# Turning the first DFT step by DMA transposes inside SBUF in a fused FFT-filter and feed-forward kernel

## The chip, the cores and the metric

The kernel runs on one NeuronCore of one Trainium2 chip. The metric is the device time of one execution in microseconds (us), as the median of several runs. The engines are named as in the profile: PE (TensorE, matrix products), PEld (its weight loads), DVE (VectorE), ACT (ScalarE), POOL (GpSimd) and SP (SyncE, which here only issues DMAs). PE writes to PSUM, from where ACT or DVE must copy the result to SBUF; this copy is called an evacuation below. Sixteen DMA engines move data between DRAM and SBUF and inside SBUF.

## The reference

Two layers, one after the other. The first is a filter in the frequency domain, the second a feed-forward layer with a squared ReLU:

```python
# x: (8, 3008, 256); w_r, w_i: (256, 256); b_r, b_i: (256,)
X = np.fft.rfft(x, axis=1)
Xr, Xi = X.real, X.imag
Yr = Xr @ w_r - Xi @ w_i + b_r
Yi = Xr @ w_i + Xi @ w_r + b_i
Yr = sign(Yr) * max(abs(Yr) - 0.01, 0)      # and Yi likewise
y = np.fft.irfft(Yr + 1j * Yi, n=3008, axis=1)

# y as 24064 tokens of 256; moe_w_in: (256, 2048); moe_w_out: (2048, 256)
h = y @ moe_w_in
g = moe_s * max(h, 0) ** 2 + moe_b
out = g @ moe_w_out
```

## The kernel before

The sequence length is split as 3008 = 94 x 32 (`N1` x `N2`), and the transform is done in two matrix products with constant tables. Per batch there are four steps, all in float16 with float32 accumulation:

- **Step 1** transforms over the 94 values of n1 to 96 rows, which the code counts by kappa (real and imaginary parts of 48 frequencies), for each of the 32 values of n2.
- **Steps 2 and 3** transform over n2 (`F_t`), multiply with the weights (`W_g`, `W_t`), shrink towards zero, and transform back over n2 (`T_t`). They need kappa and n2 together on the partitions: 24 tiles (`NPAIR`) of 128 rows (4 kappa x 32 n2) by 256 columns, held in `us`.
- **Step 4** transforms back over kappa (`C_t`). It needs the 96 kappa rows on the partitions, held in `vs`, and writes `yt`, whose partitions are the model's columns, which is what the feed-forward layer takes as its moving operand.

**Batches 1 to 7.** `s1_units(b)` is a list of 16 units. Before, a unit is one matmul of 94 x 512 with the table `A_t` as the stationary operand (L562), so that kappa comes out on the partitions, and an evacuation of 96 x 512 to `u` (L160 on ACT or L164 on DVE, as `evac` decides by counted loads). After every four units SP writes 384 KB of `u` to a DRAM tensor `ud` (L569); after the sixteenth SP reads it back in four loads with kappa and n2 on the partitions (`us`, L576). So the turn from one layout to the other is made by a trip through DRAM. `s23_units(b)` reads `us` (L598), moves the shrunk values in small copies inside SBUF (`ring`, L647), writes the result `v` to the DRAM tensor `vd` (L666) and reads it back as `vs` in two loads (L673). `s4_units(b)` reads `vs` (L710). x is loaded by POOL in four chunks per batch (`x16`, L189, four buffers), and a chunk's buffer is free again when step 1 of the batch before has read it.

**Batch 0**, in `first_batch`, goes another way, since at the opening there is no other work to lie beside. Step 1 runs with x as the stationary operand (L361), 128 columns at a time, so that the model's columns are on the partitions (`ut`). Then, for each half `ec` of the columns, come six rounds of `mix` (L410), `fwd_dft` (L441) and `inv_dft` (L459), one round behind the other. The result `vt` has the columns on the partitions, and step 4 needs kappa there: `turn` multiplies blocks of `vt` with the identity `eye_t` (L474), eight at a time, and evacuates 96 x 1024 values to `vs`. `last_dft` is step 4 of batch 0 (L491).

**The feed-forward layer** is cut into 48 tiles of tokens, each in 16 slots. A slot has two matmuls of 512 columns with `moe_w_in` (L761), the ReLU on ACT (L768), the square on DVE or ACT (L775, L772), and four matmuls of 256 columns of the tile before with `moe_w_out` (L832). The units of the four steps are put into these slots by `schedule`: step 1 and steps 2 and 3 of a batch lie in the slots of the tiles of earlier batches, about 80 to 96 slots per batch. Each engine runs its instructions in their order in the program; a matmul that waits holds up all matmuls behind it. The order inside the opening is fixed by the loop at the end of `first_batch` and rearranged a little when the program is built.

The pools set how many buffers a name has: `up` 3, `usp` 5 (each a quarter of `us`) and `vsp` 2 (each a half of `vs`) before.

Of the kernel before, what the change touches and what calls it, by code (L numbers as in the profile page):

```python
# [96 lines left out]
def kernel(  # L97
# [29 lines left out]
    sel = np.zeros((P, P))  # L127
    sel[0, :64] = 1.0
    sel[64, 64:] = 1.0
    E_d = nc.inline_tensor(np.eye(P).astype(np.float16), name="identity").ap()  # L130
    S_d = nc.inline_tensor(sel.astype(np.float16), name="bias_sel").ap()

    cpool = ctx.enter_context(tc.tile_pool(name="consts", bufs=1))
# [3 lines left out]
    fpool = ctx.enter_context(tc.tile_pool(name="psf", bufs=2, space=bass.MemoryType.PSUM))  # L137
    dpool = ctx.enter_context(tc.tile_pool(name="dram", bufs=2, space=bass.MemoryType.DRAM))
    xpool = ctx.enter_context(tc.tile_pool(name="xp", bufs=4))
    upool = ctx.enter_context(tc.tile_pool(name="up", bufs=3))  # L140
    uspool = ctx.enter_context(tc.tile_pool(name="usp", bufs=5))
    xfpool = ctx.enter_context(tc.tile_pool(name="xfp", bufs=4))
    mpool = ctx.enter_context(tc.tile_pool(name="mp", bufs=2))
    vpool = ctx.enter_context(tc.tile_pool(name="vp", bufs=3))
    vspool = ctx.enter_context(tc.tile_pool(name="vsp", bufs=2))
    ypool = ctx.enter_context(tc.tile_pool(name="yp", bufs=2))
    tpool = ctx.enter_context(tc.tile_pool(name="tp", bufs=2))
    rpool = ctx.enter_context(tc.tile_pool(name="rp", bufs=3))
# [64 lines left out]
        nc.sync.dma_start(out=st, in_=w.rearrange("(c p) e -> p c e", p=P))  # L213
        w_st.append(st)

    b_g = cpool.tile([P, 2, D], F32, name="b_g")
    nc.vector.memset(b_g, 0.0)
    for r in (0, 64):
        for i, bv in enumerate((b_r, b_i)):
            nc.sync.dma_start(out=b_g[r : r + 1, i], in_=bv.unsqueeze(0))  # L220
    F_c = uspool.tile([P, NPAIR, 2, N2], F16, name="F_c", tag="us")
    b_h = cpool.tile([P, D], F16, name="b_h")
# [4 lines left out]
    sel_t = cpool.tile([P, P], F16, name="sel_t")  # L227
    T_c = uspool.tile([P, NPAIR, 64], F16, name="T_c", tag="us")
    eye_t = cpool.tile([P, P], F16, name="eye_t")
    C_t = cpool.tile([96, 96], F16, name="C_t")  # L230

    b_st = rpool.tile([P, 2, D], F32, name="b_st", tag="rt")
# [12 lines left out]
    def emit_load_inverse():  # L245
        nc.sync.dma_start(
            out=F_c[:, H:].rearrange("p q r k -> p q (r k)"), in_=F_d[:, H:]
        )
        t_load = nc.sync.dma_start(out=T_c, in_=T_d)
        with tc.issue_after(t_load.ins):  # L250
            nc.sync.dma_start(out=eye_t, in_=E_d)
# [24 lines left out]
    F_2 = [uspool.tile([P, H, P], F16, name="F_2", tag="us") for _ in range(2)]  # L276
    for f in F_2:
        nc.gpsimd.memset(f, 0.0)

# [54 lines left out]
    def make_bias():  # L334
        ps = other_bank()
        nc.tensor.matmul(ps[:, 0:D], ones, w_sum, start=True, stop=True)
        for j in range(2):
            nc.scalar.activation(
                out=bias_bc[:, j], in_=ps[:, 0:D], func=AF.Copy, scale=bb_bc
            )  # L340

    us = {}
    vs = {}
    ring = []
# [5 lines left out]
    def first_batch():  # L350
# [46 lines left out]


        U = NPAIR // 4
        vt = bigpool.tile([P, DC, N2, 96], F16, name="vt", tag="corr")  # L400
        gs = {}
        zt = {}
        g_last = [None]
# [61 lines left out]
                ps.rearrange("p (k n) -> p n k", n=N2), 512,  # L465
            )

        for h in range(2):
            vs[(0, h)] = vspool.tile([96, HW, D], F16, name="vs", tag="vs")

        def turn(ec, k):
            ps = two_banks()
            for j in range(8):
                nc.tensor.matmul(  # L474
                    ps[0:96, j // 4, (j % 4) * P : (j % 4) * P + P],
                    vt[:, ec, 8 * k + j, :], eye_t, start=True, stop=True,
                )
            h, n = divmod(8 * k, HW)
            evac(
                vs[(0, h)][:, n : n + 8, ec * P : (ec + 1) * P],  # L480
                ps[0:96].rearrange("p h (j e) -> p (h j) e", e=P), 1024,
            )

        yt = yts[0] = ypool.tile([P, DC, N2, 96], F16, name="yt", tag="yt")

        def last_dft(ec, n2):

            ps = [one_bank(), other_bank()]
            for j in range(8):
                h, k = divmod(n2 + j, HW)  # L490
                nc.tensor.matmul(  # L491
                    ps[j // 4][:, (j % 4) * 96 : (j % 4) * 96 + 96],
                    vs[(0, h)][:, k, ec * P : (ec + 1) * P], C_t,
                    start=True, stop=True,
                )
# [14 lines left out]
        for i in range(2 * U + 2):  # L510
            if i < 2 * U:
                mix(*steps[i])
            if 0 <= i - 1 < 2 * U:
                fwd_dft(*steps[i - 1])
            if 0 <= i - 2 < 2 * U:
                inv_dft(*steps[i - 2])
            k = i - U - 2
            if 0 <= k < 4:
                turn(0, k)
            if 0 <= k - 1 < 4:  # L520
                last_dft(0, 8 * (k - 1))
            if i >= 2 * U:
                some(3)
            if i == 0:
                with tc.issue_after(g_last[0].ins):
                    place_t(0)
            if i == 1:
                with tc.issue_after(g_last[0].ins):
                    place_f(1)
            if i == 2:  # L530
                with tc.issue_after(g_last[0].ins):
                    place_f_2(1)
            if i == 3:
                with tc.issue_after(g_last[0].ins):
                    place_t(1)
            if i == 9:

                gate = nc.gpsimd.tensor_copy(out=low[0:1, 0, 0:1], in_=vt[0:1, 1, 0, 0:1])
                with tc.issue_after(gate.ins):
                    make_w_g()  # L540
                    make_bounds()
                    sum_w_out()
        for k in range(4):
            turn(1, k)
            some(1)
            if k:
                last_dft(1, 8 * (k - 1))
        last_dft(1, 24)
        return more


    def s1_units(b, more_banks=False):

        ud = dpool.tile([96, N2, D], F16, name="ud", tag="ud")
        hold = {}

        def unit(i):
            c, j = divmod(2 * i, XCH)
            if j == 0:
                hold["u"] = upool.tile([P, XCH, D], F16, name="u", tag="u")  # L560
            ps = other_bank() if more_banks and i % 2 else one_bank()
            nc.tensor.matmul(  # L562
                ps[0:96, :], A_t[0:N1, :], x16[(b, c)][0:N1, j * D : (j + 2) * D],
                start=True, stop=True,
            )
            u = hold["u"]
            evac(u[0:96, j : j + 2, :], ps[0:96, :].rearrange("p (j d) -> p j d", j=2), 512)
            if j == XCH - 2:
                nc.sync.dma_start(  # L569
                    out=ud[:, c * XCH : (c + 1) * XCH, :], in_=u[0:96]  # L570
                )
            if i == N2 // 2 - 1:
                uv = ud.rearrange("k n d -> (k n) d").rearrange("(q p) d -> p q d", p=P)
                for q in range(4):
                    t = uspool.tile([P, 6, D], F16, name="us", tag="us")
                    nc.sync.dma_start(out=t, in_=uv[:, 6 * q : 6 * q + 6, :])  # L576
                    us[(b, q)] = t

        return [lambda i=i: unit(i) for i in range(N2 // 2)]

    def s23_units(b):
# [8 lines left out]
        def fwd_unit(i):  # L590

            bank = one_bank()
            ps = bank.rearrange("p (r c j k) -> p r c j k", r=2, c=DC, j=2)
            t = us[(b, i // 3)]
            for j in range(2):
                q = (2 * i + j) % 6
                for dc in range(DC):
                    nc.tensor.matmul(  # L598
                        ps[:, :, dc, j, :], t[:, q, dc * P : (dc + 1) * P],
                        F_t[:, 2 * i + j, :], start=True, stop=True,  # L600
                    )
            xt = xfpool.tile([P, 3, DC, P], F16, name="xf", tag="xf")
# [50 lines left out]
        def inv_unit(i):  # L653
# [14 lines left out]
                )  # L668
            if i == H - 1:
                vv = vd.rearrange("q (k n) e -> (q k) (n e)", n=N2)  # L670
                for h in range(2):
                    t = vspool.tile([96, HW, D], F16, name="vs", tag="vs")
                    nc.sync.dma_start(  # L673
                        out=t.rearrange("k n e -> k (n e)"),
                        in_=vv[:, h * HW * D : (h + 1) * HW * D],
                    )
                    vs[(b, h)] = t

        units = []

# [14 lines left out]
    def s4_units(b):  # L695
# [6 lines left out]
        def unit(g):  # L702
# [3 lines left out]
            yt = yts[b]  # L706
            ps = one_bank()
            for j in range(w):
                h, k = divmod(n2 + j, HW)
                nc.tensor.matmul(  # L710
                    ps[:, j * 96 : (j + 1) * 96],
                    vs[(b, h)][:, k, ec * P : (ec + 1) * P], C_t,
                    start=True, stop=True,
                )
            evac(
# [143 lines left out]
    more = first_batch()  # L859
    load.update(act=0.0, dve=0.0)  # L860
    def load_x_2():
        emit_load_x(2, us[(1, 3)][0:1, 0, 0:1])

    mark = {}
    for i, tl in enumerate(tiles):
        if tl[0] == "main" and tl[2] == 0 or tl[0] == "wide" and tl[2] == (0, 0):
            mark[tl[1]] = i * MC
    schedule(0, 10, more)
    plan.setdefault(15, []).append(make_bias)
    plan.setdefault(17, []).append(load_x_2)  # L870
    schedule(24, 42, s23_units(1))
# [53 lines left out]
```

## Time and profile before

| | |
|---|---|
| median of 3 runs | 852.34 us (851.17 to 854.75) |
| the profiled execution's own time | 851.2 us |
| its span in the profile | 849.4 us |
| mean granted clock of PE | 0.997 |
| busy: PE, DVE, ACT, POOL | 98%, 82%, 76%, 5% |
| HBM read and written | 52.54 MB, 46.66 MB |
| batch 0's dense part (feed-forward matmuls in a row) begins | about 51.5 us |

The span is counted from the first to the last instruction of the core; the run's time is 1.8 us longer. The profile shows busy time by engine, groups of instructions by line, waits with what ended them, a timeline, the chain of work that ended last (followed back from the last instruction), and a table of stretches of time with each engine's busy time, the granted clock, the busy share of the DMA engines and the GB/s that they moved. The ends of matmuls are modelled, so a row's mean duration (382 ns for L562, 205 ns for L710) holds a latency that neighbours overlap; the pace of a run of matmuls is read from the chain.

### The profile page before, as it was taken

The page shows a single profiled execution, that of the slowest core. Times are in us where ns is not written, and L with a number is a line of the kernel's source. Part 1 is how long each engine was busy: PE and PEld are TensorE (multiplying, and loading weights), DVE is VectorE, ACT ScalarE, POOL GpSimd, SP SyncE. Part 2 cuts the span into 40 slices and gives each one's busy share as a digit, 9 for nine tenths or more (in the row PEclk, how much of TensorE's full clock was granted, in tenths as well). Part 3 has the DMA queues.
Part 4 walks back from the last instruction along what each step waited for, and adds up shares of the span by engine and source line. Part 5 has one row for each costly group of instructions (what it writes and reads, how often), then busy time and mean ns, then how long its engine had stood idle before and what let it go on. Part 6 is the DMA issues. An engine that isn't in the chain of part 4 may idle for free.

```text
span 849.4 us, 17085 instructions
## 1 busy us (share of the span) xinstructions
PE 835.0 (98%) x6645; PEld 600.5 (71%) x6645; DVE 697.0 (82%) x1027; ACT 643.2 (76%) x856; POOL 46.6 (5%) x72
## 2 busy tenths in 40 slices
PE   8899999999999999999999999999999999999997
PEld 7757777777677766777677776777667777766765
DVE  6898987888888987888878888888977888776674
ACT  5898887787778787787777887787877787766673
POOL 5321000000000000000000000000000000000000
PEclk9999999999999999999999999999999999999999
DMA  7937457324761367324662247613354223411111
GB/s 165 161 104 162 108 148 185 101 76 100 177 186 54 92 159 184 109 78 103 171 177 65 74 106 199 172 40 92 100 156 118 62 79 98 112 33 38 38 44 50
DMA packets 105458, 95.07 MB, mean 112 GB/s; under 512 B 9510, under 2 KB 97578, under 8 KB 104034
## 3 DMA queue, kind: packets, MB, share of 16 engines
q1 hardware_dynamic: 98930, 79.57, 32.6%
q0 software_dynamic: 6448, 14.42, 10.7%
q8 instruction: 52, 0.85, 0.4%
q14 instruction: 28, 0.23, 0.1%
HBM read 52.54 MB, written 46.66 MB: 117 GB/s over the span
## 4 chain that ended last, share of the span: by engine, by line
PE 88%; DVE 4%; ACT 3%; DMA 2%; issue 1%; POOL 0%; SPq 0%; DVEq 0%; ACTq 0%; POOLq 0%
PE psa L832 36%; PE psh L761 36%; PE psf L627 4%; PE psf L562 2%; PE psf L613 2%; PE psf L598 2%; PE psf L657 2%; PE psf L710 2%; ACT rt L768 1%; DVE gt L775 1%; DMA x<-in_x_dram 1%; DMA out_dram<-ost 1%; PE psh L410 1%; ACT yt L160 0%; ACT vs L160 0%
## 5 line engine op out<-in xcount | busy, mean ns | idle before, releaser
L768 ACT ACTIVATE rt<-psh 128x1024 f32<-128x1024 f32 (+2 forms) x384 | 387.1, 1009 | 119.1 <-PE psh L761 117.7
L775 DVE TENSOR_TENSOR gt<-rt 128x1024 f16<-128x1024 f32 (+2 forms) x321 | 384.0, 1199 | 98.1 <-ACT rt L768 97.4
L832 PE MATMUL psa<-w_out_t,gt 128*128 128x256 f16 (+1 forms) x3024 | 454.3, 272 | 0.1
L832 PEld LDWEIGHTS <-gt 128*128 128x128 f16 (+1 forms) x3024 | 300.9, 101 | 187.2 <-issue 1.7
L761 PE MATMUL psh<-yt,w_in 128*128 128x512 f16 (+1 forms) x1344 | 396.7, 378 | 0.3 <-ACT rt L768 0.3
L761 PEld LDWEIGHTS <-w_in 128*128 128x128 f16 x1536 | 142.9, 98 | 27.4 <-issue 2.1
L842 DVE SCALAR_TENSOR_TENSOR ost<-psa,s_bc,bias_bc 128x512 f32<-128x512 f32 (+2 forms) x97 | 71.0, 732 | 8.3 <-PE psa L832 7.1
L772 ACT ACTIVATE gt<-rt 128x1024 f16<-128x1024 f32 (+2 forms) x63 | 66.2, 1050 | 1.0
L632 DVE TENSOR_TENSOR ring<-psf,s 128x512 f16<-128x512 f32 x84 | 57.5, 684 | 3.7 <-PE psf L627 2.9
L160 ACT CAST v<-psf 128x512 f16<-128x512 f32 x78 | 45.3, 582 | 18.7 <-PE psf L657 18.7
L160 ACT CAST xf<-psf 128x512 f16<-128x512 f32 x82 | 47.9, 585 | 10.9 <-PE psf L598 10.8
L160 ACT CAST u<-psf 96x512 f16<-96x512 f32 x77 | 44.5, 580 | 11.0 <-PE psf L562 10.7
L761 PE MATMUL psh<-tail,w_in 128*128 128x512 f16 (+1 forms) x192 | 52.1, 353 | 0.0
L627 PE MATMUL psf<-W_g,xf 128*128 128x256 f16 x336 | 50.4, 273 | 0.0
L160 ACT CAST yt<-psf 128x480 f16<-128x480 f32 (+2 forms) x75 | 38.1, 520 | 13.6 <-PE psf L710 13.6
L189 POOL DMA_DIRECT2D x<-in_x_dram x36 | 18.9, 530 | 429.3 <-PE psf L562 428.0
L562 PE MATMUL psf<-x,A_t 94*96 94x512 f16 x104 | 39.7, 381 | 1.7 <-ACT yt L160 0.5
L638 DVE TENSOR_TENSOR ring<-ring,high 128x512 f16<-128x512 f16 x84 | 35.5, 423 | 2.3
L639 DVE TENSOR_TENSOR ring<-ring 128x512 f16<-128x512 f16 x84 | 35.5, 422 | 1.9
L637 DVE TENSOR_TENSOR ring<-ring,low 128x512 f16<-128x512 f16 x84 | 35.4, 421 | 1.6
L627 PEld LDWEIGHTS <-xf 128*128 128x128 f16 x336 | 32.9, 98 | 3.8
L710 PE MATMUL psf<-C_t,vs 96*128 96x96 f16 x448 | 33.0, 205 | 0.1
(89 smaller groups left out, 501.9 us busy)
## 6 DMA issues: line engine op xcount, KB each, us to landing
out_dram<-ost SPq DMA_DIRECT2D x152, 128.0 KB
ud<-u SPq DMA_DIRECT2D x28, 384.0 KB
us<-ud SPq DMA_DIRECT2D x28, 384.0 KB
vd<-v SPq DMA_DIRECT2D x42, 256.0 KB
vs<-vd SPq DMA_DIRECT2D x14, 768.0 KB
x<-in_x_dram POOLq DMA_DIRECT2D x28, 376.0 KB, 5.9
ring<-ring SPq DMA_DIRECT2D x280, 32.0 KB
out_dram<-ost SPq DMA_DIRECT2D x16, 120.0 KB
```

The lines of the kernel that those rows point to most:

```text
L160: return None, nc.scalar.copy(out=dst, in_=src)
L562: nc.tensor.matmul(ps[0:96, :], A_t[0:N1, :], x16[(b, c)][0:N1, j * D : (j + 2) * D], start=True, stop=True,)
L627: nc.tensor.matmul(ps[:, r, :], xt[:, 2 - r, dc], W_g[:, dc, r], start=(dc == 0), stop=(dc == DC - 1),)
L632: nc.vector.tensor_tensor(out=t, in0=ps, in1=hold[i // 2][:, i % 2].unsqueeze(1).to_broadcast([P, 2, D]), op=ALU.add,)
L638: nc.vector.tensor_tensor(out=m, in0=m, in1=high, op=ALU.min)
L710: nc.tensor.matmul(ps[:, j * 96 : (j + 1) * 96], vs[(b, h)][:, k, ec * P : (ec + 1) * P], C_t, start=True, stop=True,)
L761: nc.tensor.matmul(o, w_in_t[dc][:, mc * P : (mc + 1) * P], r, start=(dc == 0), stop=(dc == DC - 1),)
L768: nc.scalar.activation(out=rt[:, :, 0:w], in_=ps[:, :, 0:w], func=AF.Relu)
L772: nc.scalar.activation(out=gt[:, :, 0:w], in_=rt[:, :, 0:w], func=AF.Square)
L775: nc.vector.tensor_tensor(out=gt[:, :, 0:w], in0=rt[:, :, 0:w], in1=rt[:, :, 0:w], op=ALU.mult)
L832: nc.tensor.matmul(ps[0:size, h, :], gts[(ti, mc // 2)][:, mc % 2, sub * size : (sub + 1) * size], w_out_t[:, mc, :], start=(mc == 0), sto ...
L842: nc.vector.scalar_tensor_tensor(out=ost[0:size, 0:k], in0=ps[0:size, 0:k], scalar=s_bc[0:size], in1=bias_bc[0:size, 0:k], op0=ALU.mult, o ...
```

## The change

Two places change, and the pools with them.

First, step 1 of batches 1 to 7 takes the form that batch 0 has: x is the stationary operand, four matmuls of 94 x 96 per unit, so that the columns come out on the partitions. A unit now covers four values of n2 and one half `dc` of the columns; the first eight units do the first half, the last eight the second, and each half reads all four chunks of x. `u` holds for each column all 96 x 32 values with kappa outside and n2 inside. After each half, one DMA transpose inside SBUF turns 128 x 3072 values into the 24 tiles of `us`. The DRAM tensor `ud` is gone.

Second, batch 0's `turn` is two DMA transposes of 128 x 2048 values for each half of the columns instead of identity matmuls and evacuations. `vt` is padded to 128 rows for this, and POOL zeroes the padding once. In the loop, `last_dft` of the first half stands three rounds behind the turn; all twelve units of step 1 of batch 1 stand between the second half's turn and its `last_dft`, and the last four between the calls of `last_dft`, so that no unit is left for the slots of the first tile.

The buffers: `us`, `u` and `vs` have one buffer each, for a whole batch; the constants of the opening share the space of `us`, and the bias tables that of `tails`.

```diff
-    E_d = nc.inline_tensor(np.eye(P).astype(np.float16), name="identity").ap()
...
-    upool = ctx.enter_context(tc.tile_pool(name="up", bufs=3))
-    uspool = ctx.enter_context(tc.tile_pool(name="usp", bufs=5))
+    upool = ctx.enter_context(tc.tile_pool(name="up", bufs=1))
+    uspool = ctx.enter_context(tc.tile_pool(name="usp", bufs=1))
...
-    vspool = ctx.enter_context(tc.tile_pool(name="vsp", bufs=2))
+    vspool = ctx.enter_context(tc.tile_pool(name="vsp", bufs=1))
...
+    first_c = uspool.tile([P, 4, NPAIR * 64], F16, name="first_c", tag="us")
+    F_c = first_c[:, 0].rearrange("p (q r k) -> p q r k", q=NPAIR, r=2)
+    T_c = first_c[:, 1].rearrange("p (q k) -> p q k", q=NPAIR)
+    F_2 = [first_c[:, 2 + i].rearrange("p (q k) -> p q k", q=H) for i in range(2)]
...
+    vt = bigpool.tile([P, DC, N2, P], F16, name="vt", tag="corr")
+    nc.gpsimd.memset(vt[:, :, :, 96:P], 0.0)
...
-        def turn(ec, k):
-            ps = two_banks()
+        vs[0] = vspool.tile([P, N2, D], F16, name="vs", tag="vs")
+
+        def turn(ec):
+
+            for k in range(2):
+                nc.sync.dma_start(
+                    out=vs[0][:, HW * k : HW * k + HW, ec * P : (ec + 1) * P],
+                    in_=vt[:, ec, HW * k : HW * k + HW].rearrange("p n k -> p (n k)"),
+                    transpose=True,
+                )
...
             for j in range(8):
                 nc.tensor.matmul(
-                    ps[0:96, j // 4, (j % 4) * P : (j % 4) * P + P],
-                    vt[:, ec, 8 * k + j, :], eye_t, start=True, stop=True,
-                )
-            h, n = divmod(8 * k, HW)
-            evac(
-                vs[(0, h)][:, n : n + 8, ec * P : (ec + 1) * P],
-                ps[0:96].rearrange("p h (j e) -> p (h j) e", e=P), 1024,
-            )
...
-            k = i - U - 2
-            if 0 <= k < 4:
-                turn(0, k)
-            if 0 <= k - 1 < 4:
-                last_dft(0, 8 * (k - 1))
-            if i >= 2 * U:
-                some(3)
+            if i - 1 in (U, 2 * U):
+                turn((i - 1) // U - 1)
+            if 0 <= i - U - 4 < 4:
+                last_dft(0, 8 * (i - U - 4))
...
+        some(12)
         for k in range(4):
-            turn(1, k)
+            last_dft(1, 8 * k)
             some(1)
-            if k:
-                last_dft(1, 8 * (k - 1))
-        last_dft(1, 24)
...
-            ps = other_bank() if more_banks and i % 2 else one_bank()
-            nc.tensor.matmul(
-                ps[0:96, :], A_t[0:N1, :], x16[(b, c)][0:N1, j * D : (j + 2) * D],
-                start=True, stop=True,
-            )
+            for j in range(4):
+                lo = (4 * h + j) * D + dc * P
+                nc.tensor.matmul(
+                    ps[:, j * 96 : j * 96 + 96], x16[(b, c)][0:N1, lo : lo + P],
+                    A_t[0:N1, :], start=True, stop=True,
+                )
...
-                nc.sync.dma_start(
-                    out=ud[:, c * XCH : (c + 1) * XCH, :], in_=u[0:96]
-                )
-            if i == N2 // 2 - 1:
-                uv = ud.rearrange("k n d -> (k n) d").rearrange("(q p) d -> p q d", p=P)
-                for q in range(4):
-                    t = uspool.tile([P, 6, D], F16, name="us", tag="us")
-                    nc.sync.dma_start(out=t, in_=uv[:, 6 * q : 6 * q + 6, :])
-                    us[(b, q)] = t
+                nc.sync.dma_start(
+                    out=us[b][:, :, dc * P : (dc + 1) * P],
+                    in_=u[:, dc].rearrange("p k n -> p (k n)"),
+                    transpose=True,
+                )
...
-    schedule(0, 10, more)
+    assert not more
```

More of the change, by code (lines that the diff above doesn't have):

```diff
@@ L214 @@
         w_st.append(st)
-    b_g = cpool.tile([P, 2, D], F32, name="b_g")
+    b_g = tpool.tile([P, 2, D], F32, name="b_g", tag="tail")
     nc.vector.memset(b_g, 0.0)
@@ L220 @@
             nc.sync.dma_start(out=b_g[r : r + 1, i], in_=bv.unsqueeze(0))
-    F_c = uspool.tile([P, NPAIR, 2, N2], F16, name="F_c", tag="us")
-    b_h = cpool.tile([P, D], F16, name="b_h")
+    first_c = uspool.tile([P, 4, NPAIR * 64], F16, name="first_c", tag="us")
+    F_c = first_c[:, 0].rearrange("p (q r k) -> p q r k", q=NPAIR, r=2)
+    T_c = first_c[:, 1].rearrange("p (q k) -> p q k", q=NPAIR)
+    F_2 = [first_c[:, 2 + i].rearrange("p (q k) -> p q k", q=H) for i in range(2)]
+    sb_t = tpool.tile([P, P + D], F16, name="sb_t", tag="tail")
+    sel_t, b_h = sb_t[:, 0:P], sb_t[:, P:]
     nc.vector.memset(b_h, 0.0)
@@ L226 @@
         nc.gpsimd.dma_start(out=b_h[64 * i : 64 * i + 1], in_=bv.unsqueeze(0))
-    sel_t = cpool.tile([P, P], F16, name="sel_t")
-    T_c = uspool.tile([P, NPAIR, 64], F16, name="T_c", tag="us")
-    eye_t = cpool.tile([P, P], F16, name="eye_t")
     C_t = cpool.tile([96, 96], F16, name="C_t")
@@ L250, in emit_load_inverse @@
         with tc.issue_after(t_load.ins):
-            nc.sync.dma_start(out=eye_t, in_=E_d)
             nc.sync.dma_start(out=C_t, in_=C_d)
@@ L275 @@
     nc.vector.memset(T_t, 0.0)
-    F_2 = [uspool.tile([P, H, P], F16, name="F_2", tag="us") for _ in range(2)]
     for f in F_2:
@@ L399, in first_batch @@
         U = NPAIR // 4
-        vt = bigpool.tile([P, DC, N2, 96], F16, name="vt", tag="corr")
         gs = {}
@@ L466, in inv_dft @@
             )
-        for h in range(2):
-            vs[(0, h)] = vspool.tile([96, HW, D], F16, name="vs", tag="vs")
-        def turn(ec, k):
-            ps = two_banks()
-            for j in range(8):
-                nc.tensor.matmul(
-                    ps[0:96, j // 4, (j % 4) * P : (j % 4) * P + P],
-                    vt[:, ec, 8 * k + j, :], eye_t, start=True, stop=True,
-                )
-            h, n = divmod(8 * k, HW)
-            evac(
-                vs[(0, h)][:, n : n + 8, ec * P : (ec + 1) * P],
-                ps[0:96].rearrange("p h (j e) -> p (h j) e", e=P), 1024,
-            )
+        vs[0] = vspool.tile([P, N2, D], F16, name="vs", tag="vs")
[5 more added lines that the diff above has]
+                    transpose=True,
+                )
         yt = yts[0] = ypool.tile([P, DC, N2, 96], F16, name="yt", tag="yt")
@@ L489, in last_dft @@
             for j in range(8):
-                h, k = divmod(n2 + j, HW)
                 nc.tensor.matmul(
                     ps[j // 4][:, (j % 4) * 96 : (j % 4) * 96 + 96],
-                    vs[(0, h)][:, k, ec * P : (ec + 1) * P], C_t,
+                    vs[0][0:96, n2 + j, ec * P : (ec + 1) * P], C_t,
                     start=True, stop=True,
@@ L542, in first_batch @@
                     sum_w_out()
+        some(12)
         for k in range(4):
-            turn(1, k)
+            last_dft(1, 8 * k)
             some(1)
-            if k:
-                last_dft(1, 8 * (k - 1))
-        last_dft(1, 24)
         return more
     def s1_units(b, more_banks=False):
-        ud = dpool.tile([96, N2, D], F16, name="ud", tag="ud")
         hold = {}
         def unit(i):
-            c, j = divmod(2 * i, XCH)
-            if j == 0:
-                hold["u"] = upool.tile([P, XCH, D], F16, name="u", tag="u")
-            ps = other_bank() if more_banks and i % 2 else one_bank()
-            nc.tensor.matmul(
-                ps[0:96, :], A_t[0:N1, :], x16[(b, c)][0:N1, j * D : (j + 2) * D],
-                start=True, stop=True,
-            )
-            u = hold["u"]
-            evac(u[0:96, j : j + 2, :], ps[0:96, :].rearrange("p (j d) -> p j d", j=2), 512)
-            if j == XCH - 2:
+            dc, g = divmod(i, N2 // 4)
+            if i == 0:
+                hold["u"] = upool.tile([P, DC, 96, N2], F16, name="u", tag="u")
+                us[b] = uspool.tile([P, NPAIR, D], F16, name="us", tag="us")
+            c, h = divmod(g, 2)
+            ps = other_bank() if more_banks and i % 2 else one_bank()
+            for j in range(4):
[4 more added lines that the diff above has]
+                )
+            u = hold["u"]
+            evac(
+                u[:, dc, :, 4 * g : 4 * g + 4],
+                ps[:, 0:384].rearrange("p (n k) -> p k n", k=96), 384,
+            )
+            if g == N2 // 4 - 1:
@@ L593, in fwd_unit @@
             ps = bank.rearrange("p (r c j k) -> p r c j k", r=2, c=DC, j=2)
-            t = us[(b, i // 3)]
             for j in range(2):
-                q = (2 * i + j) % 6
                 for dc in range(DC):
                     nc.tensor.matmul(
-                        ps[:, :, dc, j, :], t[:, q, dc * P : (dc + 1) * P],
+                        ps[:, :, dc, j, :], us[b][:, 2 * i + j, dc * P : (dc + 1) * P],
                         F_t[:, 2 * i + j, :], start=True, stop=True,
@@ L670, in inv_unit @@
                 vv = vd.rearrange("q (k n) e -> (q k) (n e)", n=N2)
+                t = vs[b] = vspool.tile([P, N2, D], F16, name="vs", tag="vs")
                 for h in range(2):
-                    t = vspool.tile([96, HW, D], F16, name="vs", tag="vs")
                     nc.sync.dma_start(
-                        out=t.rearrange("k n e -> k (n e)"),
+                        out=t[0:96, h * HW : h * HW + HW].rearrange("k n e -> k (n e)"),
                         in_=vv[:, h * HW * D : (h + 1) * HW * D],
                     )
-                    vs[(b, h)] = t
         units = []
@@ L708, in unit @@
             for j in range(w):
-                h, k = divmod(n2 + j, HW)
                 nc.tensor.matmul(
                     ps[:, j * 96 : (j + 1) * 96],
-                    vs[(b, h)][:, k, ec * P : (ec + 1) * P], C_t,
+                    vs[b][0:96, n2 + j, ec * P : (ec + 1) * P], C_t,
                     start=True, stop=True,
@@ L861, in load_x_2 @@
     def load_x_2():
-        emit_load_x(2, us[(1, 3)][0:1, 0, 0:1])
+        emit_load_x(2, us[1][0:1, 0, 0:1])
     mark = {}
```

## The prediction

> **What bounds the kernel now.** I read the chain of work that ended last first. It says which engine a saved instruction must sit on to be worth anything.
>
> ```profile
> PE 88%; DVE 4%; ACT 3%; DMA 2%; issue 1%; POOL 0%; SPq 0%; DVEq 0%; ACTq 0%; POOLq 0%
> ```
>
> PE carries 88% of the end, DMA 2%. So the first step's trip through DRAM (`ud`, `us`), which the change removes, costs nothing today; only PE work counts there. What that work costs is read from the chain in order of time, where neighbours do not overlap:
>
> ```profile
> 51.21 0.22 PE psf L562
> ...
> 243.69 0.43 PE psf L710 x10
> ```
>
> A first-step matmul over 512 columns takes 0.22 us (217 ns over many). The last step's 96-column matmul, with a weight load for each, goes ten in 0.43 us, 43 ns each: the shape that the changed first step will have.
>
> The windows of the opening come next, since batch 0 has nothing beside it to hide in:
>
> ```profile
> 8.00:12.00 4.00, 3.66 (x43) 3.55 (x42) 1.92 (x5) 2.52 (x6) 2.75 (x3) 0.57 1.10 200
> ...
> 28.00:32.00 4.00, 3.86 (x48) 3.22 (x47) 2.73 (x5) 3.59 (x6) 0.00 (x0) 1.00 1.08 216
> 32.00:36.00 4.00, 3.72 (x55) 3.42 (x53) 3.47 (x5) 3.32 (x6) 3.06 (x4) 1.00 1.36 193
> 36.00:40.00 4.00, 3.93 (x60) 3.55 (x58) 3.77 (x6) 3.41 (x7) 2.68 (x4) 1.00 0.71 96
> ```
>
> The last column but one is the DMA share: the 16 DMA engines are full until about 39 us (the weights of the second part and batch 1's x), just when batch 0's first turn will be asked for. The column before it is the granted clock; after the waits on x it fell to 0.57.
>
> Last, the timeline of SP and PE in batch 3's first step, for what a transpose may take before somebody waits:
>
> ```profile
> 241.88 0.31 SPq L569 DMA_DIRECT2D ud<-u  x1
> ...
> 247.67 2.55 SPq L576 DMA_DIRECT2D us<-ud  x4
> ```
> ```profile
> 253.26 0.39 PE L598 MATMUL psf<-F_t,us 128*128 128x128 f16 x4
> ```
> ```profile
> 250.00:255.00 5.00, 5.00 (x41) 3.72 (x39) 3.85 (x4) 3.27 (x5) 0.70 (x1) 1.00 0.95 268
> ```
>
> From the end of the first step to the first reader of `us` are 11.4 us (12.2 in batch 2, 16 to 18 in others). The window is the reload of `us` in 512-byte pieces: 268 GB/s at 95%.
>
> **The first step of batches 2 to 7.** Out: 16 matmuls of 217 ns, 3.47 us. In: 64 of 43 ns, 2.75 us. Gain 0.72 us a batch, 4.3 us for six, all on PE. The evacuations shrink from 582 to 479 ns on ScalarE and from 681 to 558 on VectorE (rows of `u` now and of batch 0's `ut`, which has the new form); neither is the bound. The DRAM copies go, worth nothing.
>
> **The price of a DMA transpose.** No row of before shows one. Below: as fast as the fastest copy, 268 GB/s, so 2.0 us for one of batch 0's four (128 x 2048, 524 KB) and 2.9 us for one of a later batch's two (128 x 3072, 786 KB). Middle: each 128-element row of a block is a piece of its own and costs what a 512-byte piece costs in that window, 16 x 512 B / 268 GB/s = 30.6 ns on one of 16 engines: 128 pieces, 3.9 us, and 192 pieces, 5.9 us. Above: each such row cut in eight, 31 and 47 us. I take the middle, because the pieces of a transpose must be at least as many as those of the plain copy nearest to it, and keep both ends. To each comes some 2 us from issue to landing that bytes don't explain (the `vd` write of 256 KB issued at 222.4 us was waited for until 226.6, of which 1 us is bytes; I take less, as that one had a queue ahead).
>
> The page "DMA: Bandwidth & Descriptors" of the Trainium skill, section "Latency and other measured facts", gives 261 GB/s for a DMA transpose; by it the lower end holds. The page "VectorE: DVE Perf Modes", section "The three transpose paths", speaks against the change: 1309 ns for a 128 x 128 block by DMA against 390 on TensorE, and it prefers TensorE where PSUM will do. Block after block that would be 21 and 31 us, and a total beyond 1000 us as an estimate. Here TensorE turned eight blocks in 0.46 us (`turn` L474 in the chain), 57 ns each, plus an evacuation of 1.0 to 1.2 us for the eight.
>
> **Batch 0, the opening.** The 64 identity matmuls and eight evacuations go (about 8.5 us of ScalarE and VectorE together); an opening step falls from 2.4 to 1.73 us (the inverse matmuls stand at 26.33, 28.06 and 29.79 us before any turn, then 31.75, 34.19, 36.54). By the order of the changed program the first reader of the turned rows stands after three more such steps: 29.79 + 3 x 1.73 + 0.2 = 35.2 us. The transpose is issued when the last `vt` is written, 31.45 us. With the engines full until 39.6 us (when POOL's wait for `w_out_t` at L327 ends) and shared with the weights, 3.9 us become about 7, and with 2 us the first half lands at 40.8: PE, in order, stands 5.6 us with the rest of the opening behind it. The second half: 46.5 us, against 44.8 when PE gets there, 1.7 more. Then the last `vt` at 47.7, the other transposes from there, landing at 53.6 and 57.5. Twelve units of batch 1's first step cover 3.3 us of it (12 evacuations of 0.48 and 0.56 on two engines), so PE waits from 51.0 to 53.6 and, after 1.5 us of work, from 55.1 to 57.5; 1.5 us more and the dense part begins at 59.0. Before, it ran from 51.5. That is +7.5 us. Six first-step units that lay in the first tile move ahead of it; the tile is paced by ScalarE, three of its 0.6 us evacuations go: -1.8. The stalls should cost clock too (the 0.57 window): I take +1.0. Opening: +6.7 us.
>
> **What is newly late in the dense part.** Two things. The old order read a chunk of x once, so the next batch's load could start after four units; the new one reads each chunk again for the second half of the columns, so all four loads (4.1 to 10.4 us each, off the path today: POOL's wait for L562 is 428 us and nobody waits for POOL) crowd into the second half of the step, beside the `vs` reload (issued 226.6, read from 236.2 us) and the second transpose. And the first transpose stands on SP ahead of the last two `vd` writes and the `vs` reload, which wait behind its 5.9 us. The second has 2 + 5.9 = 7.9 us against 11.4: it fits, unless it shares the engines with a load (13.8, 2 us late in batches 2 and 3). I charge 1.0 for that and 1.5 for `vs`. `us`, `u` and `vs` with one buffer cost nothing: their last readers are over 10 us back; if the transposes grew past 9 us, that cover would go first.
>
> The rest is free: the extra memset of `vt` on POOL (some 2 us by the 1.4 us row of 1536 columns) ends before POOL's gate at 16.7 us; the constants in other pools move no copy that is waited for.
>
> **Sum.** -4.3 + 6.7 + 1.0 + 1.5 = +4.9 on the profiled run's own 851.2 us (span 849.4): 856.1. The median of the runs is 1.1 above that run: 857.
>
> **Rivals.** (1) Transposes at copy speed, faster: the lower end. First half at 31.45 + 2 + 4 = 37.5, second at 43.6, the other two at 48.8 and 50.8, dense part from 52.3: +0.8 - 1.8 = -1.0; in the dense part nothing is late but 0.5; total -4.8, so 847.5 by the median. For it: 268 GB/s is reached by 512-byte pieces here. Against: a transpose scatters each piece over partitions. (2) The weights hold the DMA engines and copy speed gives back only PE's gain less the stall: no change, 849 to 855; it decides where one of batch 0's transposes takes about 3 us. (3) The transposes are long and become the bound: at 8 us (12 for a later batch) the opening adds about 25 us and each batch some 2, 885 us; past 11 us for a later one, `vs` and `us` are late in every batch by twice the excess, and at 31 and 47 us the total is some 1300. For it: a 16-bit transpose writes short runs. Against: no row. That the change does not do what it says is out: the changed program has four transposes of 128x16x128 and fourteen of 128x24x128 on SP, no identity matmul and no `ud`.
>
> **How the numbers follow.** About 0.5% is what a measurement here tells from no change, so 848.1 to 856.6 us is "same". My forecast (slower by 4 to 15 us) 0.38, rival 1 0.28, rival 2 0.20, rival 3 0.14. Slower 0.52, same 0.20, faster 0.28; the forecast's own range is 856 to 867. The whole reaches from 843 (copy speed and no stall) to 890 (rival 3's beginning), and leaves out its long end and a little below.
>
> **What would show it.** In the changed profile: DMA waits of the reader of `vs` in `last_dft` between 35 and 58 us, some 10 us of them; PE under 8 tenths in the second slice; the first-step line at 43 ns each; in the dense part at most 2 us of PE waits on `us` and `vs`. I am wrong if the opening shows no PE wait on a DMA (rival 1) or if such waits come in every batch (rival 3).

## The result, and the profile after

The changed kernel takes 884.43 us as a median of four runs (882.15 to 890.61), the kernel before, beside it, 852.05 us: a ratio of 1.0386, 95% interval 1.0326 to 1.0446. That is 32.4 us slower. The profiled execution of after took 886.09 us with a span of 884.3.

The chain by engine, on after's page, in answer to the first line shown of before:

```profile
PE 83%; DMA 10%; ACT 3%; issue 2%; DVE 1%; POOL 1%; SPq 0%; DVEq 0%; ACTq 0%; POOLq 0%
```

DMA has gone from 2% to 10% of the end. Which transfers those are stands in the waits of PE (engine, line and tile, what it waited for: us in total, times, longest):

```profile
PE psf L589 <- DMA us<-u: 17.9, 3, 10.6
PE psf L486 <- DMA vs<-vt: 11.4, 3, 7.5
```

`vs<-vt` are the opening's transposes, `us<-u` those of the later batches. The prediction had some 10 us of the first kind and at most 2 us of the second. The chain in order of time gives the pace of the new first step, and beside it the longest transfer:

```profile
63.94 24.98 DMA us<-u
...
122.48 0.17 PE psf L556 x4
```

Four matmuls in 0.17 us are 43 ns each, as worked out. But batch 1's second transpose, 786 KB, was on the chain for 25 us. PE's timeline shows who waited (start, duration, then in brackets the wait before it and its releaser):

```profile
43.68 0.50 PE L486 MATMUL psf<-C_t,vs 96*128 96x96 f16 x4 [7.54 <-DMA vs<-vt]
...
56.46 0.50 PE L486 MATMUL psf<-C_t,vs 96*128 96x96 f16 x4 [1.70 <-DMA vs<-vt]
...
60.75 0.50 PE L486 MATMUL psf<-C_t,vs 96*128 96x96 f16 x4 [2.19 <-DMA vs<-vt]
...
88.97 0.82 PE L589 MATMUL psf<-F_t,us 128*128 128x128 f16 x6 [10.55 <-DMA us<-u]
```

The other two waits on `us` are in batch 4, 3.62 us at 373.43 and 3.72 at 377.44. The windows by 4 us of the two stretches (PE, PEld, DVE, ACT, POOL busy, granted clock, DMA share, GB/s):

```profile
36.00:40.00 4.00, 0.14 (x3) 0.00 (x0) 0.00 (x0) 1.24 (x3) 2.77 (x4) 0.77 1.38 157
40.00:44.00 4.00, 0.32 (x5) 0.32 (x6) 0.00 (x0) 0.00 (x0) 2.76 (x3) 0.50 1.30 135
44.00:48.00 4.00, 4.00 (x34) 3.35 (x32) 2.56 (x4) 1.38 (x3) 3.77 (x4) 0.50 0.26 58
...
68.00:72.00 4.00, 4.00 (x22) 2.04 (x21) 4.00 (x4) 3.81 (x6) 0.00 (x0) 1.00 1.40 78
72.00:76.00 4.00, 4.00 (x26) 2.28 (x24) 4.00 (x5) 3.05 (x4) 0.00 (x0) 1.00 1.11 76
...
84.00:88.00 4.00, 0.00 (x0) 0.00 (x0) 0.00 (x0) 0.00 (x0) 0.00 (x0) 0.50 0.45 69
```

From 68 to 76 us the DMA engines are booked beyond full (1.40, 1.11) and move 76 to 78 GB/s, less than a third of the 268 GB/s of the plain reload before. What shares them stands in the timelines of POOL and SP:

```profile
64.24 2.18 POOL L188 DMA_DIRECT2D x<-in_x_dram  x4 [0.31 <-POOL x L184]
```
```profile
63.94 3.61 SPq L566 DMA_TRANSPOSE us<-u  x1
```

All four loads of batch 2's x start within 3 us of the second transpose. Before, they waited for the last quarter of `us` and began at 69.81, with the reload over:

```profile
68.97 0.64 POOL L185 COPY x<-us 1x1 f16<-1x1 f16 x4 [20.01 <-DMA us<-ud]
69.81 2.19 POOL L189 DMA_DIRECT2D x<-in_x_dram  x4 [0.20 <-POOL x L185]
```

The change rewrote that gate (a one-element copy from `us` on POOL ahead of each load), `emit_load_x(2, us[(1, 3)][0:1, 0, 0:1])` to `emit_load_x(2, us[1][0:1, 0, 0:1])`, and column 0 of the new `us` belongs to the first transpose.

Undisturbed, a transpose is short. After's windows, 2 us in batch 0's second turn and 1 us in batch 3's first transpose:

```profile
54.00:56.00 2.00, 0.71 (x12) 0.56 (x11) 0.96 (x2) 1.24 (x3) 0.00 (x0) 0.80 1.13 208
```
```profile
242.00:243.00 1.00, 1.00 (x12) 0.72 (x10) 1.00 (x2) 1.00 (x2) 0.00 (x0) 1.00 1.14 217
```

At 208 and 217 GB/s, 524 KB take 2.5 us and 786 KB 3.6 us, 19 ns for each 256-byte piece on one of 16 engines. That the pieces are rows of a block is in the packet counts: 60246 under 512 B where before had 9510, which is 50736 more, and the transposes have 14 x 3072 + 4 x 2048 = 51200 such rows.

### The profile page after: what moved, and what is told of

Its sections match the earlier page's. It is cut to its first block, busy times and chain, and to the rows that moved or that the text cites. A ratio compares the mean times of both kernels' runs of the same rounds, so it can differ in the third digit from the quotient of the medians.

```text
span 884.3 us, 17541 instructions
## 1 busy us (share of the span) xinstructions
PE 838.5 (95%) x6917; PEld 609.7 (69%) x6917; DVE 691.5 (78%) x1019; ACT 635.3 (72%) x856; POOL 47.7 (5%) x73
## 2 busy tenths in 40 slices
DMA packets 132004, 86.16 MB, mean 97 GB/s; under 512 B 60246, under 2 KB 126810, under 8 KB 130578
## 4 chain that ended last, share of the span: by engine, by line
PE 83%; DMA 10%; ACT 3%; issue 2%; DVE 1%; POOL 1%; SPq 0%; DVEq 0%; ACTq 0%; POOLq 0%
PE psa L821 34%; PE psh L750 34%; DMA us<-u 5%; PE psf L618 4%; PE psf L589 2%; DMA vs<-vt 2%; PE psf L604 2%; PE psf L648 2%; PE psf L699 2%; PE psf L556 2%; ACT rt L757 1%; DMA vs<-vd 1%; DMA vd<-v 1%; DMA x<-in_x_dram 1%; DMA first_c<-dft_inv 0%
## 5 line engine op out<-in xcount | busy, mean ns | idle before, releaser
L750 PE MATMUL psh<-yt,w_in 128*128 128x512 f16 (+1 forms) x1344 | 401.6, 381 | 0.0
L750 PEld LDWEIGHTS <-w_in 128*128 128x128 f16 x1536 | 138.8, 99 | 15.7 <-issue 1.8
L159 ACT CAST xf<-psf 128x512 f16<-128x512 f32 x81 | 47.3, 585 | 29.3 <-PE psf L589 29.2
L761 ACT ACTIVATE gt<-rt 128x1024 f16<-128x1024 f32 (+2 forms) x64 | 67.5, 1054 | 1.0
L589 PE MATMUL psf<-F_t,us 128*128 128x128 f16 x336 | 33.4, 223 | 17.9 <-DMA us<-u 17.9
L159 ACT CAST u<-psf 128x384 f16<-128x384 f32 x82 | 39.3, 481 | 12.9 <-PE psf L556 11.9
L159 ACT CAST yt<-psf 128x480 f16<-128x480 f32 (+2 forms) x73 | 37.1, 524 | 14.5 <-PE psf L699 13.7
L595 DVE TENSOR_TENSOR xf<-xf 128x256 f16<-128x256 f16 x84 | 23.7, 287 | 22.8 <-ACT xf L159 22.3
L589 PEld LDWEIGHTS <-us 128*128 128x128 f16 x336 | 26.2, 100 | 20.9 <-DMA us<-u 18.6
```

Source lines behind the costliest of these rows:

```text
L159: return None, nc.scalar.copy(out=dst, in_=src)
L589: nc.tensor.matmul(ps[:, :, dc, j, :], us[b][:, 2 * i + j, dc * P : (dc + 1) * P], F_t[:, 2 * i + j, :], start=True, stop=True,)
L750: nc.tensor.matmul(o, w_in_t[dc][:, mc * P : (mc + 1) * P], r, start=(dc == 0), stop=(dc == DC - 1),)
L761: nc.scalar.activation(out=gt[:, :, 0:w], in_=rt[:, :, 0:w], func=AF.Square)
```

## The experiments

The theory, A: short transposes become long only where loads from another queue run beside them, and the rest of the loss is the opening. The first rival, B: the transposes are long by themselves, and whatever reads `us` waits. A second, C: SP's own plain copies in line with the transposes hold them.

**Batch 2's x behind the second transpose** (column `P` of `us` belongs to it):

```diff
-        emit_load_x(2, us[1][0:1, 0, 0:1])
+        emit_load_x(2, us[1][0:1, 0, P : P + 1])
```

> The load of batch 2's x now waits for the second transpose of batch 1's us instead of the first. Theory A (a DMA transpose is quick by itself, some 4 us for 786 KB, and becomes many times slower when POOL's casting loads of x are in flight with it): the second transpose lands some 6 us after its issue at 64 us instead of 25, the 10.6 us wait of PE at 78 us goes, with the half clock behind it; 872 us. Theory B (a transpose of a whole half is slow by its own descriptors, whatever else is in flight): the reader still waits until about 89 us; 884 us as the changed kernel.

870.94 us, ratio 1.0223 [1.0206, 1.0240]: 13.5 us of the 32.4 come back, as A says. In POOL's timeline the loads now start when the transpose has landed,

```profile
75.02 2.19 POOL L188 DMA_DIRECT2D x<-in_x_dram  x4
```

and batch 1's wait is gone; PE waits 5.7 us on `us`, in batch 4. One after the other, transpose (issued at 65.1, landed 70.7) and loads are done earlier than side by side (88.9).

**The same for every batch**, on top of that:

```diff
-            plan.setdefault(s1 + 6, []).append(lambda b=b: emit_load_x(b + 1))
+            plan.setdefault(s1 + 6, []).append(lambda b=b: emit_load_x(b + 1, us[b][0:1, 0, P : P + 1]))
```

> As the run before, and every later batch's load of x waits for the second transpose of the batch before. Theory A: batch 4's wait for us (7.3 us of PE wait, 13 us in the shift of the later steps) goes as well; 859 us, and the rest of the loss is the opening's turn. Theory B: 884 us. A third theory (plain copies of SP, the reload of vs above all, slow a transpose as much as POOL's loads do): batch 4 stays late, about 872 us.

860.73 us, 1.0108 [1.0093, 1.0123]: another 10.2 us. PE's list begins with the opening's waits, and none on `us` is left:

```profile
PE psf L486 <- DMA vs<-vt: 13.3, 3, 9.1
```

SP's plain copies are as they were, so C falls. The gain is more than the 5.7 us of waits on `us`. PE's busy time fell too, from 835.9 us to 830.9, as the granted clock around batch 4 (0.72 to 0.94 between 350 and 370 us in the run before) is 1.00 here; and a wait of 1.7 us on the reload of `vs` is gone.

**The dense part alone, ungated.** Batch 0 turned by identity products as before, step 1 of batches 1 to 7 by transposes:

```diff
+        def turn(ec, k):
+            ps = two_banks()
+            for j in range(8):
+                nc.tensor.matmul(
+                    ps[0:96, j // 4, (j % 4) * P : (j % 4) * P + P],
+                    vt[:, ec, 8 * k + j, :], eye_t, start=True, stop=True,
...
+            evac(
+                vs[0][0:96, 8 * k : 8 * k + 8, ec * P : (ec + 1) * P],
...
```

> Only the first step of batches 1 to 7 is changed; batch 0 is turned by identity products as before, and the gates of x are those of the changed kernel. If the loss splits by place: theory A gives late us in batch 1 (about 12 us) and batch 4 (13 us) less 5 us of PE work: 872 us. If the opening's turn were the whole loss: 847 us.

858.76 us, 1.0083 [1.0068, 1.0098]: a miss by 13 us. PE waits 8.1 us on `us`, and batch 1 has only 1.78 of it. With the opening's old order batch 1's first transpose is issued at 47.3 us, and the loads of batch 2's x start from 54.2 to 56.8, ahead of the second transpose:

```profile
56.51 9.40 SPq L576 DMA_TRANSPOSE us<-u  x1
```
```profile
60.00:64.00 4.00, 4.00 (x28) 2.44 (x26) 4.00 (x5) 2.82 (x3) 0.00 (x0) 1.00 1.07 192
```

Here the same loads and the same transpose share the engines at 174 to 200 GB/s, and PE is released at 67.98, 11.5 us after the issue. The trace also keeps the start and length of every DMA packet: the transpose's first 256-byte packet starts at 60.6 us, when the loads have moved 0.81 of their 1.54 MB. So most of the 13.5 us of batch 2's gate seem to need the opening's new order too, in which transpose and loads start together; a load beside a transpose is not always so dear.

**The opening alone**, on the kernel before: `turn(ec)` by two transposes into the halves of `vs`, `vt` padded, the new order of `first_batch`, and `up` with 2 buffers for 3 to make room:

```diff
+                nc.sync.dma_start(
+                    out=vs[(0, k)][:, :, ec * P : (ec + 1) * P],
+                    in_=vt[:, ec, HW * k : HW * k + HW].rearrange("p n k -> p (n k)"),
+                    transpose=True,
+                )
```

> Only batch 0's turn is changed; batches 1 to 7 go through DRAM as before (u with two buffers instead of three, to make room). The opening's PE waits for vs (11.4 us in the changed kernel) and the half clock during them remain, nothing else: 863 us. If the opening's turn were covered, 852 us; if it were the whole loss, 888 us.

868.84 us, 1.0201 [1.0186, 1.0216], 5.8 us over what was expected. Two waits, in PE's list:

```profile
PE psf L485 <- DMA vs<-vt: 9.3, 1, 9.3
PE psa L485 <- ACT u L159: 5.9, 1, 5.9
```

The first is the first turn. The second is this kernel's own: the old step 1 writes `u` to `ud` by SP behind the transposes, and with two buffers an evacuation waits for it. So this run bounds the price of the opening from above; the next gives it.

**The dense part alone with both gates.** The identity products of the run before last and the gates of the second:

> The first step of batches 1 to 7 by DMA transposes with every load of x behind the second transpose of the batch before; batch 0 turned by identity products. If the loads of x were all that made the transposes late, what is left is the gain on PE (0.72 us a batch) and the smaller evacuations: 846 us, faster than before. If the transposes cost something of their own in the dense part (the queue ahead of vs): 852 us or more.

847.09 us, 0.9945 [0.9933, 0.9958]: faster than the kernel before by 4.8 us, and than the changed one by 37. PE waits nowhere on `us`, and its busy time is 4.3 us under the 835.0 of the kernel before. Section 1 of its page, span 845.3:

```profile
PE 830.7 (98%) x6981; PEld 607.9 (72%) x6981; DVE 693.9 (82%) x1025; ACT 639.0 (76%) x858; POOL 52.7 (6%) x92
```

Against the gated kernel with the transposed opening (860.73) the opening, its new order included, costs 13.6 us. The four terms, 13.5 + 10.2 + 13.6 - 4.8, make 32.5. They are steps along one path from the changed kernel to the one before, and so must add up; along another the split differs. With the old opening both gates together are worth 11.7 us (858.76 to 847.09), not 23.7, and without the gates the opening costs 25.7 (884.43 to 858.76).

**Control: the gates alone on the kernel before.**

```diff
-            plan.setdefault(s1 + 6, []).append(lambda b=b: emit_load_x(b + 1))
+            plan.setdefault(s1 + 6, []).append(lambda b=b: emit_load_x(b + 1, us[(b, 3)][0:1, 0, 0:1]))
```

> The kernel before, with nothing changed but the loads of x of batches 3 to 7, which wait for the last part of us as in e5_dense_gated. If e5's gain is the new form of the first step: 852 us here. If it came from moving the loads of x out of the way of other copies: about 847 us.

852.05 us, 1.0006 [0.9997, 1.0015]. The gates by themselves give nothing, so the 4.8 us come from the new form of step 1 and what goes with it.

**`w_out` out of the first turn's way**, on the fully gated kernel: its load waits for the second transpose of the first turn.

```diff
+        gate = nc.gpsimd.tensor_copy(out=w_out_t[0:1, 0, 0:1], in_=first)
...
+                if i - 1 == U:
+                    emit_load_w_out(vs[0][0:1, HW, 0:1])
```

> As e2_gate_all, and the load of w_out waits for the second transpose of batch 0's first turn instead of running beside it. If the casting loads make that turn long, its first half lands at about 37 us instead of 45, PE's wait of 9.1 us falls to some 2, and the half clock behind it goes: 851 us. If the turn is long by itself: 860 us.

856.01 us, 1.0048 [1.0035, 1.0062]: 4.7 us better, not the 10 hoped for. PE's timeline:

```profile
36.93 0.34 PE L490 MATMUL psf<-C_t,vs 96*128 96x96 f16 x4 [1.59 <-DMA vs<-vt]
...
54.01 0.50 PE L490 MATMUL psf<-C_t,vs 96*128 96x96 f16 x4 [7.55 <-DMA vs<-vt]
```

With the engines to itself the first half lands 5.7 us after its issue at 31.19 and PE waits 1.6 us for it. Then `w_out`, started at 41.4, meets the second turn, and that waits 7.55 us. The collision has moved, not gone.

**The clock kept up** in the same gated kernel, by matmuls that nobody reads, in the waits of the opening:

```diff
+                with tc.issue_after(pe_last[0].ins):
+                    awake = keep_awake(150)
...
+                    awake = keep_awake(40)
```

> As e2_gate_all, with 150 idle matmuls on PE ahead of the first last_dft and twice 40 ahead of the third and the fifth part, so that PE is busy while it would wait for the turned rows. If the low granted clock after the waits is a real part of the opening's loss: no windows at 0.5 there, and about 4 us less, 856 us. If the clock costs nothing because the engines that evacuate set the pace there: 860 us.

857.83 us, 1.0071 [1.0055, 1.0086], 2.9 us better: what the slow clock after the waits costs at least, since the idle matmuls may delay a reader themselves. The window of this kernel that answers to after's 40 to 44:

```profile
40.00:44.00 4.00, 4.00 (x76) 4.00 (x73) 0.00 (x0) 0.00 (x0) 1.14 (x1) 1.00 1.11 134
```

**What about the loads makes them so dear?** Three runs, each of one execution. Batch 2's x becomes a constant in float16, in plain copies (POOL's loads convert from float32), started when the first transpose of batch 1 has landed; later batches are ungated. First, 94 rows from ScalarE's queue:

```diff
+            gate = nc.gpsimd.tensor_copy(out=t[0:1, 0:1], in_=us[1][0:1, 0, 0:1])
+            nc.scalar.dma_start(out=t[0:N1, :], in_=X_d[c])
```

> The changed kernel with batch 2's x loaded as float16 by plain copies of the same landed bytes from ScalarE's queue (a constant in x's place), gated as in the changed kernel, so that they run beside the second transpose of batch 1. If any concurrent copy slows a transpose: the reader of us still waits until 85 us or later. If it is POOL's casting loads that do: the transpose lands before 74 us and PE's wait on us at batch 1 goes.

898.67 us; the second transpose took longer still, 29.8 us from its issue at 64.26 to its reader, with one window in the middle of it at 73 GB/s, and PE waited 26.54 us:

```profile
76.00:80.00 4.00, 0.00 (x0) 0.00 (x0) 0.00 (x0) 0.00 (x0) 0.00 (x0) 0.50 1.28 73
```
```profile
94.01 0.82 PE L592 MATMUL psf<-F_t,us 128*128 128x128 f16 x6 [26.54 <-DMA us<-u]
```

Part of this wait is the order of the program: the reader stands earlier here, and PE reached it at 67.5 us, in the changed kernel at 78.4. So the landing is what can be compared, and it is later than there. A conversion is not needed, then, to hold a transpose for so long. It is not cleared either, for these copies do not run as POOL's loads do. By the packets of the traces 1.9 of the copies' 4096-byte packets are under way at a time on the mean, and they move 48 GB/s from 66.5 to 98.8 us; POOL's loads of the same 94 rows have 11 packets under way beside the transpose of the changed kernel and 14.5 when no transpose runs beside them (in the run with batch 2's gate alone). The copies go out two at a time, so the transpose meets another kind of neighbour. Then the same with 96 rows (`out=t[0:96, :]`):

> As e8_plain_x, but the constant in place of batch 2's x has 96 rows instead of 94, so that its copies can be spread over all 16 DMA engines as those of the other tiles are. If what slowed the transpose in e8 was any copy from a second queue beside it: the reader of us waits until 85 us or later again. If it was the odd row count of those copies: the transpose lands before 74 us and no wait of PE on us is left at batch 1; the time falls to about 872 us.

896.57 us in all, with further waits in batches 2 and 4; batch 1 is where the question lies:

```profile
68.00:72.00 4.00, 0.79 (x5) 0.27 (x3) 2.27 (x3) 2.30 (x3) 0.00 (x0) 0.91 1.19 238
```
```profile
79.74 0.82 PE L592 MATMUL psf<-F_t,us 128*128 128x128 f16 x6 [10.95 <-DMA us<-u]
```

The transpose landed 14.2 us after its issue at 65.5, neither the 74 us nor the 85 of the two expectations; PE had reached the reader at 68.8, early as in the run before. Now 9.3 of the copies' packets are under way at a time, and for 8 us the engines move 228 to 238 GB/s: what the row count changed is how many packets of a copy run side by side. The transpose still shares them with 1.57 MB of copies. Last, 96 rows from SP, in the transposes' own queue (`nc.sync.dma_start`):

> As e9_plain96, with the four copies issued by SP behind the transpose, in the same queue. If the order within one queue protects a transpose: it lands before 74 us, no wait at batch 1, about 872 us. If any bytes in flight beside it slow it, whatever the queue: a wait as in e9_plain96.

881.45 us. At batch 1 there is no wait on `us`, with the engines at 262 GB/s:

```profile
68.00:72.00 4.00, 4.00 (x22) 2.00 (x21) 4.00 (x4) 3.81 (x6) 0.00 (x0) 1.00 1.02 262
```
```profile
78.11 0.50 PE L592 MATMUL psf<-F_t,us 128*128 128x128 f16 x6
```

The missing wait alone would not show it: the reader stands late again, and a transpose that took 14.2 us from its issue at 64.06 would have held PE for only 0.1 us. The packets do: the transpose's run from 65.2 to 69.0 us, as fast as alone, and the copies' from 69.0 to 75.2, after it. So the same bytes behind the transpose and not beside it did not slow it. The total still missed the expected 872, for its ungated batches 2 and 4 wait 16.9 us.

## Why the prediction was right or wrong

It said slower, and it is; the 884.43 us lie within the range. But the sum was +4.9 and +32.4 was measured; the time fell out of the forecast's own range (856 to 867) and onto the number of rival 3 (885), by another mechanism than that rival named. That the range holds it is luck: its upper end was drawn for transposes that are long by themselves, and they are short.

**The first step** held: 43 ns a matmul, evacuations of 481 ns on ScalarE and 553 on VectorE for 479 and 558, and a gain of 4.8 us where 4.3 was worked out. The DRAM trip was off the path, as read: with it gone, hardly more came back than PE's own gain.

**The price of a transpose** was over-sized. I took 3.9 and 5.9 us; alone they cost 2.5 and 3.6 plus about 2 us of landing, near the lower end. Rival 1 was right on that and lost all the same. The skill's two figures stand thus: "DMA: Bandwidth & Descriptors", section "Latency and other measured facts", has 261 GB/s for the non-contiguous case, and 208 to 217 were measured here. The 1309 ns per block of "VectorE: DVE Perf Modes", section "The three transpose paths", is not borne out as a rate: 16 blocks in 2.5 us are 0.16 us each. That page's advice to use TensorE where PSUM will do (section "Rules for kernel authors") is borne out for the opening, by 13.6 us.

**The opening** was named rightly and under-sized, +6.7 against +13.6. The first half came when the reader had stood 7.54 us, not 5.6 (43.68 against 40.8): from issue to landing 9.4 us were counted, 7 of them for sharing with the weights, and 11.7 passed (5.7 with `w_out` out of the way). The other waits summed to 3.9 for 6.7. The dense part begins at 62.0 us, not 59.0, and the clock term is at least 2.9, not 1.0. Those two are 3.0 and 1.9 of the 6.9 us missing, and overlap in part. The rest, and whether the credit of 1.8 us for the first tile came in, no run separates.

**The step that failed** is in "newly late in the dense part": "it fits, unless it shares the engines with a load (13.8, 2 us late in batches 2 and 3)", charged 1.0 us. It cost 23.7 (13.5 + 10.2) beside the new opening, and 11.7 beside the old. Two errors are in it. The sum took sharing as addition, 7.9 + 5.9; with the four loads started beside it the transpose took 25 us, since the engines together moved 76 GB/s. And the place was wrong: the loads were looked for in the second half of step 1, while the rewritten gate at L851 is what let batch 2's x start with the second transpose of batch 1. The full diff has that line, the excerpt ahead of the prediction leaves it out, and the sum has no term for it. It was batches 1 and 4 that waited, not 2 and 3.

**The `vs` term** of 1.5 us is not seen: PE waits 0.3 us on the reload. `us`, `u` and `vs` with one buffer cost nothing seen either.

What stays open: why POOL's loads, with 11 packets under way, held the transpose for 25 us, and 96-row plain copies, with 9, for 14 (the conversion from float32, the row count and the queue all differ); why loads that start 2 us ahead of it are milder (192 GB/s) than those that start with it (76); and why, ungated, it is batch 4 of the later ones that waits.

## What to carry to other kernels

A DMA that replaces engine work is priced twice: alone, and beside whatever its neighbours in other queues have under way; the second can be several times the first and is not a sum. When a change merges buffers, read every gate that names one: a wait that stays correct may now wait for an earlier event and start a transfer on top of the one it used to follow. Take the parts of a change apart: here one half gained 4.8 us, and holding back the loads of x and leaving the opening as it was kept it.

## What the runs showed of the hardware

- A 786 KB transpose in SBUF at 217 GB/s alone (3.6 us) took 25 us from issue to reader beside four 94-row converting loads from POOL's queue that started with it, and 11.5 beside those that started just ahead of it. It took 30 us beside four 94-row plain copies from ScalarE's queue (73 GB/s) and 14 us beside 96-row ones (238 GB/s). With those behind it in its own queue its last packet was done 5 us after its issue.
- Of a 94-row plain copy from ScalarE's queue 1.9 packets were under way at a time on the mean (48 GB/s), of a 96-row one 9.3 beside the transpose and, from SP's queue, 14.9 behind it (253 GB/s). POOL's 94-row converting loads had 14.5 with no transpose beside them.
- After PE had stood in a wait for 7.5 us the granted clock was 0.50 and stayed there for some 4 us of full work (44 to 48 us); keeping PE busy through the opening's waits was worth 2.9 us.
